# The sign of the gate and value weights: from ScalarE to VectorE

## The chip, the core and the metric
The kernel runs on one core of a Trainium2 chip. TensorE (PE) multiplies matrices; VectorE (DVE), ScalarE (ACT) and GpSimd (POOL) do elementwise work; SyncE (SP) issues the transfers. Each engine takes its instructions strictly in the order of its own program, and waits on semaphores for the others. The metric is the device time of one execution in microseconds (us), lower is better.

## The reference
Three stages follow one another, with `S` = 576 positions, 8 heads of 64, batch 4, thus 2304 tokens of 512:

```python
scores = scale * (q @ k.T);  keep the 32 largest of each row;  attn = softmax of these;  x = attn @ v
x = ((1 / (1 + exp(-(x @ w_gate)))) * (x @ w_val)) @ w_out      # 512 -> 1536 -> 512
h = x @ w_in;  r = maximum(h, 0);  out = (r * r) @ w_out2       # 512 -> 2048 -> 512
```

`q`, `k`, `v` are float32. The five weights come as float64, and there is no float64 arithmetic on the engines: the kernel makes float32 of the two 32-bit words of each number by bit operations.

## The kernel before
**Attention.** The tokens are cut into row blocks of 128; a unit is one head of one block (144 in all). TensorE makes the scores (`sp`), ScalarE copies them (`S`), VectorE finds the 32 largest by four MAX8 (line 389) with three MATCH_REPLACE8 (line 396) between them, ScalarE makes the exponentials (lines 408, 424), VectorE the reciprocal of the sum (`rz`, line 429), TensorE transposes (`tp`, `tq`) and multiplies by the values (`xp`). The first two blocks are chunks 0 and 1, which go through both layers in float32 (`moe32`); later chunks use float16 halves of the weights (`split`).

**Weights.** `conv` takes pairs of 128x512 blocks, 34 pairs: 6 each of gate (`wg`), value (`wv`) and out (`wo`) weights, then 8 each of `wi` and `w2`. For each block: ScalarE scales the high word to float32 (`c`, line 607); VectorE shifts both blocks of `c` by three bits (line 609); ScalarE makes the low word's share (`low`, line 613); the sign is put in; GpSimd adds `low` to `c` (line 623). The sign is put in one of two ways. In a pair whose number divided by `SGN` = 3 leaves 1, ScalarE writes the high word as a float16 zero with its sign into the upper half of `low` (line 616), and the add brings it into `c`. In the other pairs VectorE takes the sign bit out of the high word and ORs it into `c` (line 620). Pairs 1, 4, 7, ... 34 go by ScalarE: two of `wg`, two of `wv`, two of `wo`, three of `wi`, three of `w2`.

**The first MoE step.** When `x_plain` of chunk 0 is there, TensorE makes gate and value of it (`pg`, line 905), ScalarE the tanh (line 914), GpSimd a scale (line 915), VectorE the product `g` (line 917), and TensorE multiplies `g` by the out weights (`acc`, line 927). Beside it run the matmuls of line 640 (`wg_n`: a norm of the weights).

**Order.** Priorities (written into `tc.cur_priority`) and a timeline of estimated durations decide at build time in which order the instructions of each engine stand; the chip then follows that order. So a change of one instruction can move others, on every engine, to the end of the program.

Of the kernel before, what the change touches and what calls it, by code (L numbers as in the profile page):

```python
# [47 lines left out]
SM2 = ()  # L48
XUP = 1000
DIAG = 2  # L50
SGN = 3
SGNS = (1,)
M4RAW = 0
# [21 lines left out]
def tile_topk_attention__then__two_moe_layers(  # L75
# [206 lines left out]
    class Pair:  # L282
# [97 lines left out]
        def softmax(self, j, i, ss, late=None):  # L380
# [48 lines left out]
            nc.vector.reciprocal(rz, bs[:, 3:4])  # L429
            if self.ci < DIAG:  # L430
                dg = apool.tile([P, P], F32, tag="we", bufs=3, name=f"dg_{tt}_{h}")
# [27 lines left out]
        def transpose(self, j, i, wk, dg):  # L459
# [8 lines left out]
            for c in range(CB):  # L468
                o, x = tp[:, c * P : (c + 1) * P], wk[:, c * P : (c + 1) * P]
                if self.ci < DIAG:  # L470

# [3 lines left out]
            nc.scalar.copy(ptr[:, :, i * P : (i + 1) * P], tp.rearrange("p (c t) -> p c t", c=CB))  # L475
            if self.ci < DIAG:
                if i == 0 and j == 0:
# [82 lines left out]
    nblk = [0]  # L560
# [5 lines left out]
    def fetch_to(i):  # L566
        while fetched[0] < len(blocks):
            b = fetched[0]
            spare = b >= len(blocks) - M4RAW
            if b > i and not (b <= i + PREF and (spare or live[0] + 3 <= WSLOTS)):  # L570
                break
            n, kt, fb = blocks[b]
            src = weights[n][kt * P : (kt + 1) * P, fb * 512 : (fb + 1) * 512]
            pool, kw = (mpool, {"tag": "m4", "bufs": M4}) if spare else (wpool, {"tag": "w"})
            if src.dtype == F32:
                t = pool.tile([P, 512], F32, name=f"{n}_r{kt}_{fb}", **kw)
                nc.sync.dma_start(t, src)
            else:
                t = pool.tile([P, 512, 2], U32, name=f"{n}_r{kt}_{fb}", **kw)
                nc.sync.dma_start(t.rearrange("p f t -> p (f t)"), src.bitcast(U32))  # L580
            if not spare:
                live[0] += 1
            raws[(n, kt, fb)] = t
            fetched[0] += 1

    def conv(name, pi):

        pr = pairs_of[name][pi]
        fetch_to(blocks.index((name, *pr[-1])))
        if (name, pi) in CM4:  # L590
            c = mpool.tile([P, 2, 512], F32, tag="m4", bufs=M4, name=f"{name}_c{pi}")
        else:
            c = wpool.tile([P, 2, 512], F32, tag="w", name=f"{name}_c{pi}")
            live[0] += 1
        rs = [raws.pop((name, kt, fb)) for kt, fb in pr]
        ci = c.bitcast(U32)
        wide = weights[name].dtype != F32
        for e, r in enumerate(rs):
            nblk[0] += 1
            if not wide:  # L600
                nc.gpsimd.tensor_copy(c[:, e], r)
            elif YMOD and nblk[0] % YMOD == 0:
                nc.gpsimd.tensor_scalar(
                    c[:, e], r.bitcast(F32)[:, :, 1], REBIAS, 1.0, op0=ALU.mult, op1=ALU.mult
                )
            else:
                nc.scalar.activation(c[:, e], r.bitcast(F32)[:, :, 1], AF.Copy, scale=REBIAS)
        if wide:
            nc.vector.tensor_scalar(ci, ci, 3, None, op0=ALU.logical_shift_left)
            for e, r in enumerate(rs):  # L610
                hi = r[:, :, 1]
                low = r[:, :, 0].bitcast(I32)
                nc.scalar.activation(low, r[:, :, 0], AF.Copy, scale=float(2.0**-29))
                if nblk[0] // 2 % SGN in SGNS:

                    nc.scalar.activation(
                        r.bitcast(F16)[:, :, 1], hi.bitcast(F32), AF.Copy, scale=float(2.0**-60)
                    )
                else:
                    nc.vector.scalar_tensor_tensor(  # L620
                        ci[:, e], hi, 0x80000000, ci[:, e], op0=ALU.bitwise_and, op1=ALU.bitwise_or
                    )
                nc.gpsimd.tensor_tensor(
                    c.bitcast(I32)[:, e], c.bitcast(I32)[:, e], low, op=ALU.add
                )
        live[0] -= sum(blocks.index((name, *b)) < len(blocks) - M4RAW for b in pr)
        for e, (kt, fb) in enumerate(pr):
            flat[(name, kt, fb)] = (c, e)
# [42 lines left out]
    def weight_step(n=1):  # L671
        for _ in range(min(n, len(steps) - nstep[0])):
            name, pi = steps[nstep[0]]
            conv(name, pi)
            nstep[0] += 1
# [607 lines left out]
```

## Time and profile before

| | us |
|---|---|
| median of 3 runs (lowest to highest) | 1274.77 (1273.74 to 1278.67) |
| the profiled execution: its time | 1270.1 |
| its span in the trace | 1267.8 |
| TensorE busy in the span | 1171.9 |
| VectorE, GpSimd, ScalarE busy | 956.3, 844.9, 830.0 |

The profile is that of one execution. The span leaves out some 2.3 us of start and end. A busy time counts an instruction from its start in the record to its end, with what it stalled inside; the records of neighbours overlap a little. A row of a wait names who waited, and after the arrow who came last.

### The profile page before, as it was taken

Reading aid. Unit: us, or ns where it says so; the run is one execution under the profiler, and the core shown is the slowest. Engines: PE = TensorE matmul, PEld = TensorE weight load, DVE = VectorE, ACT = ScalarE, POOL = GpSimd, SP = SyncE. Lnnn points to the kernel's source line nnn. Section 1 sums busy time; section 2 is a strip of 40 time slices with the busy share of each in tenths; the row PEclk is TensorE's granted clock in tenths of the full one; section 3 lists DMA queues with packets and bytes.
Section 4 is the critical chain, followed back from the end, with each engine's and each line's share of the span. In section 5 each row is a group of like instructions: output and inputs, shape, how many; then the busy total and the mean of one; then the engine's idle time right before and its main releaser. Section 6 shows DMA issues by size and latency. Waiting matters only on the chain.

```text
span 1267.8 us, 30670 instructions
## 1 busy us (share of the span) xinstructions
PE 1171.9 (92%) x11477; PEld 952.5 (75%) x11477; DVE 956.3 (75%) x1965; ACT 830.0 (65%) x1719; POOL 844.9 (67%) x1294
## 2 busy tenths in 40 slices
PE   6657889999889989899998999999999999999998
PEld 5436877987777868779786778877886887787775
DVE  6998789899789868889997788998999969210010
ACT  4998996577676766667766676776676757322122
POOL 1788774488776576777875887797688749515223
PEclk9667999999989999999997999999999999999999
DMA  6988763223354346665667465466544623200000
GB/s 183 366 293 284 259 191 85 57 78 88 109 151 118 95 93 147 147 134 119 146 128 155 99 164 120 119 138 154 105 101 92 126 48 67 55 1 1 18 1 17
DMA packets 243188, 153.92 MB, mean 121 GB/s; under 512 B 193120, under 2 KB 209504, under 8 KB 243040
## 3 DMA queue, kind: packets, MB, share of 16 engines
q1 hardware_dynamic: 243040, 151.97, 47.1%
q8 instruction: 90, 1.47, 0.5%
q14 instruction: 58, 0.48, 0.1%
HBM read 105.51 MB, written 18.09 MB: 97 GB/s over the span
## 4 chain that ended last, share of the span: by engine, by line
PE 62%; DVE 14%; ACT 9%; DMA 7%; POOL 5%; issue 3%; SPq 1%; DVEq 0%; POOLq 0%; ACTq 0%
PE ph L851 11%; PE acc L872 10%; PE pv L747 7%; PE pg L747 7%; PE acc L787 6%; PE sp L374 6%; DVE mx L389 5%; DVE W L396 5%; PE xp L506 2%; PE ph L952 2%; DMA PT<-S 2%; DMA kst<-ks 2%; PE acc L969 2%; PE xp L533 2%; PE qpt L334 1%
## 5 line engine op out<-in xcount | busy, mean ns | idle before, releaser
L389 DVE MAX8 mx<-W 128x8 f32<-128x576 f32 x432 | 327.9, 759 | 11.1
L396 DVE MATCH_REPLACE8 W<-mx,W 128x576 f32<-128x576 f32 x288 | 213.8, 742 | 0.0
L851 PE MATMUL ph<-x,wi_w 128*128 128x256 f16 (+1 forms) x1920 | 190.7, 252 | 4.6 <-ACT x L825 3.6
L872 PE MATMUL acc<-w_w,rh 128*128 128x512 f16 x768 | 181.8, 379 | 2.2 <-POOL rh L864 2.2
L851 PEld LDWEIGHTS <-wi_w 128*128 128x128 f16 x1920 | 156.4, 98 | 30.6 <-issue 5.2
L747 PE MATMUL pv<-xs,wv_w 128*128 128x256 f16 (+1 forms) x1440 | 147.0, 254 | 6.0 <-DVE th L759 4.8
L747 PE MATMUL pg<-xs,wg_w 128*128 128x256 f16 (+1 forms) x1440 | 148.2, 253 | 3.1 <-ACT xs L520 2.2
L374 PE MATMUL sp<-kst,qt 128*128 128x288 f32 x608 | 135.3, 335 | 15.7 <-DMA kst<-ks 8.8
L408 ACT ACTIVATE W<-S,mx 128x576 f32<-128x576 f32 x144 | 111.8, 776 | 51.7 <-DVE mx L389 51.4
L454 POOL TENSOR_TENSOR S<-W,S 128x512 f16<-128x512 f32 x192 | 137.0, 736 | 1.6
L747 PEld LDWEIGHTS <-wv_w 128*128 128x128 f16 x1440 | 117.9, 99 | 22.1 <-issue 9.2
L747 PEld LDWEIGHTS <-wg_w 128*128 128x128 f16 x1440 | 118.6, 99 | 17.4 <-issue 1.0
L377 ACT COPY S<-sp 128x576 f32<-128x576 f32 x144 | 92.0, 639 | 57.3 <-PE sp L374 37.5
L872 PEld LDWEIGHTS <-rh 128*128 128x128 f16 x768 | 72.5, 98 | 74.0 <-POOL rh L864 2.8
L787 PEld LDWEIGHTS <-wo_w 128*128 128x128 f16 x1440 | 117.9, 98 | 12.6 <-issue 0.8
L389 DVE MAX8 mx<-S 128x8 f32<-128x576 f32 x144 | 107.3, 745 | 25.0 <-ACT S L377 25.0
L759 DVE TENSOR_TENSOR th<-pv,th 128x512 f32<-128x512 f32 (+1 forms) x60 | 34.5, 576 | 121.3 <-PE pv L747 113.9
L374 PEld LDWEIGHTS sp<-kst,qt 128*128 128x128 f32 x608 | 92.4, 196 | 27.8 <-DMA kst<-ks 8.0
L452 POOL TENSOR_SCALAR W<-W,rz 128x576 f32<-128x576 f32 x96 | 71.9, 749 | 59.8 <-ACT S L451 57.4
L863 POOL TENSOR_TENSOR r<-r 128x512 f32<-128x512 f32 (+1 forms) x80 | 69.6, 871 | 57.4 <-ACT rh L862 51.8
L451 ACT ACTIVATE S<-W,rz 128x576 f16<-128x576 f32 x96 | 74.2, 774 | 50.4 <-DVE rz L447 47.1
L396 DVE MATCH_REPLACE8 W<-mx,S 128x576 f32<-128x576 f32 x144 | 106.9, 743 | 0.3 <-issue 0.3
(290 smaller groups left out, 2349.6 us busy)
## 6 DMA issues: line engine op xcount, KB each, us to landing
kst<-ks SPq DMA_DIRECT2D x112, 288.0 KB, 3.2
v<-vd SPq DMA_DIRECT2D x32, 320.0 KB, 3.4
qn<-in_q_dram SPq DMA_DIRECT2D x128, 64.0 KB, 2.4
wi_r<-in_moe_w_in_dram SPq DMA_DIRECT2D x16, 512.0 KB, 6.1
w_r<-in_moe_w_out_dram SPq DMA_DIRECT2D x16, 512.0 KB, 4.5
v<-in_v_dram SPq DMA_DIRECT2D x56, 128.0 KB, 2.4
wg_r<-in_moe_w_gate_dram SPq DMA_DIRECT2D x12, 512.0 KB, 6.4
wv_r<-in_moe_w_val_dram SPq DMA_DIRECT2D x12, 512.0 KB, 7.0
```

The costliest lines, as they stand in the source:

```text
L374: nc.tensor.matmul(sp[:, e, 0:HALF], l, r, start=(x == 0), stop=(x == len(ops) - 1))
L377: nc.scalar.copy(ss.rearrange("p (e s) -> p e s", e=2), sp[:, :, 0:HALF])
L389: m8 = nc.vector.max(mx[:, r], cur)
L396: nc.vector.match_replace(wk, mx[:, r], cur, NEG)
L408: nc.scalar.activation(wk, ss, AF.Prelu, bias=kth, scale=-1.0, alpha=1.0 / BIG)
L451: nc.scalar.activation(pp[:, 0:S], wk, AF.Copy, scale=rz)
L452: nc.gpsimd.tensor_scalar(wk, wk, rz, 1.0, op0=ALU.mult, op1=ALU.mult)
L454: nc.gpsimd.tensor_tensor(pp[:, o : o + e - f], wk[:, f:e], pp[:, f:e], op=ALU.subtract)
L747: nc.tensor.matmul(pp[:, e * N : (e + 1) * N], wblk(wd, a, c, f0, P), xs[:, b_, c, :], start=(e == 0 and n == 0), stop=(n == 3 * KM - 1), ...
L787: nc.tensor.matmul(accs[d // 2][:, (d % 2) * N : (d % 2 + 1) * N], wblk("wo", a, f, d * P, P), gh[:, b_, e * N : (e + 1) * N], start=(f == ...
L851: nc.tensor.matmul(ph[:, e * N : (e + 1) * N], wblk("wi", a, c, f0, P), x2[:, b_, c, :], start=(e == 0 and n == 0), stop=(n == 3 * KM - 1) ...
L872: nc.tensor.matmul(acc2[i][:, 0:DM], gh[:, b_, e * N + i * P : e * N + (i + 1) * P], wblk("w2", a, f, 0, DM), start=(f == 0 and x == 0), s ...
```

## The change
The sign by ScalarE (line 616 before, 617 after) is kept to the names in a new constant, `wo`, `wi` and `w2`. The four pairs of `wg` and `wv` that had it, eight blocks, take the VectorE way, line 620 before, 621 after.

```diff
--- before.py
+++ after.py
@@ -48,6 +48,7 @@
 SM2 = ()
 XUP = 1000
 DIAG = 2
+SGNW = ("wo", "wi", "w2")
 SGN = 3
 SGNS = (1,)
 M4RAW = 0
@@ -611,7 +612,7 @@
                 hi = r[:, :, 1]
                 low = r[:, :, 0].bitcast(I32)
                 nc.scalar.activation(low, r[:, :, 0], AF.Copy, scale=float(2.0**-29))
-                if nblk[0] // 2 % SGN in SGNS:
+                if name in SGNW and nblk[0] // 2 % SGN in SGNS:
 
                     nc.scalar.activation(
                         r.bitcast(F16)[:, :, 1], hi.bitcast(F32), AF.Copy, scale=float(2.0**-60)
```

ScalarE has eight instructions fewer and VectorE eight more; every other instruction of the program is there as before. All five engines' orders differ in many places from there on. Line numbers of the changed kernel are higher by one.

The first place is VectorE's queue at the first pair of gate weights, in the fourth unit of chunk 0's attention (`wg_c` is the float32 pair, `wg_r` the raw words, `mx`, `S` and `W` the unit's tiles). Before:

```order
L389 MAX mx_3_467<-S_3_327 128x8
L609 TENSOR_SCALAR wg_c_217<-wg_c_217 128x1024
L396 MATCH_REPLACE W_3_466<-mx_3_467,S_3_327 128x576
L389 MAX mx_3_467<-W_3_466 128x8
L396 MATCH_REPLACE W_3_466<-mx_3_467,W_3_466 128x576
L389 MAX mx_3_467<-W_3_466 128x8
```

After:

```order
L390 MAX mx_3_467<-S_3_327 128x8
L610 TENSOR_SCALAR wg_c_217<-wg_c_217 128x1024
L397 MATCH_REPLACE W_3_466<-mx_3_467,S_3_327 128x576
L621 SCALAR_TENSOR_TENSOR wg_c_217<-wg_r_0_205,wg_c_217 128x512
L621 SCALAR_TENSOR_TENSOR wg_c_217<-wg_r_0_207,wg_c_217 128x512
L390 MAX mx_3_467<-W_3_466 128x8
L174 TENSOR_TENSOR kl_3_419<-kpt_3_0_420,kp_3_418 128x512
```

Two sign instructions stand in the softmax of that unit, ahead of its second MAX.

The second place is VectorE's queue ahead of the first product `g` of chunk 0's MoE (`mx_2`, `W_2` are the third unit of chunk 1, `wi_c_1233` and `wi_c_1247` the second and third pairs of `wi`). Before:

```order
L389 MAX mx_2_1121<-S_2_996 128x8
L609 TENSOR_SCALAR wi_c_1233<-wi_c_1233 128x1024
L396 MATCH_REPLACE W_2_1120<-mx_2_1121,S_2_996 128x576
L620 SCALAR_TENSOR_TENSOR wi_c_1233<-wi_r_0_1032,wi_c_1233 128x512
L620 SCALAR_TENSOR_TENSOR wi_c_1233<-wi_r_0_1034,wi_c_1233 128x512
L917 TENSOR_TENSOR g_0_962<-pg_0_942,th_0_959 128x256
L389 MAX mx_2_1121<-W_2_1120 128x8
L173 TENSOR_TENSOR kn_1_964<-kpt_1_0_970,kp_1_969 128x512
L917 TENSOR_TENSOR g_1_1066<-pg_1_1046,th_1_1063 128x256
```

After:

```order
L621 SCALAR_TENSOR_TENSOR wi_c_1233<-wi_r_0_1032,wi_c_1233 128x512
L621 SCALAR_TENSOR_TENSOR wi_c_1233<-wi_r_0_1034,wi_c_1233 128x512
L390 MAX mx_2_1121<-W_2_1120 128x8
L430 RECIPROCAL rz_1_1027<-bs_1_1023 128x1
L397 MATCH_REPLACE W_2_1120<-mx_2_1121,W_2_1120 128x576
L610 TENSOR_SCALAR wi_c_1247<-wi_c_1247 128x1024
L390 MAX mx_2_1121<-W_2_1120 128x8
L174 TENSOR_TENSOR kn_1_964<-kpt_1_0_970,kp_1_969 128x512
L174 TENSOR_TENSOR kn_1_964<-kpt_1_4_977,kp_1_969 128x64
L621 SCALAR_TENSOR_TENSOR wi_c_1247<-wi_r_1_1068,wi_c_1247 128x512
L621 SCALAR_TENSOR_TENSOR wi_c_1247<-wi_r_1_1070,wi_c_1247 128x512
L918 TENSOR_TENSOR g_0_962<-pg_0_942,th_0_959 128x256
```

The rest of that unit's softmax (three MAX, two MATCH_REPLACE), a reciprocal, two key subtractions and the third pair of `wi` (line 609, twice line 620) now stand ahead of `g_0`; they stood behind it.

The third place is TensorE's queue at the first multiplication by the out weights, which reads that `g_0`. Before:

```order
L905 MATMUL pg_1_1046<-x_plain,wv_c_502 128x128 x2
L905 MATMUL pg_1_1046<-x_plain,wv_c_574 128x128 x2
L905 MATMUL pg_1_1046<-x_plain,wv_c_502 128x128 x2
L905 MATMUL pg_1_1046<-x_plain,wv_c_574 128x128 x2
L165 MATMUL kpt_1_0_970<-ident,kn_1_964 128x128 x4
L165 MATMUL kpt_1_4_977<-ident,ke_1_967 128x64
L927 MATMUL acc_0_1198<-g_0_962,wo_c_752 128x128
L640 LDWEIGHTS wg_c_217
```

After:

```order
L166 MATMUL kpt_1_0_970<-ident,kn_1_964 128x128 x4
L166 MATMUL kpt_1_4_977<-ident,ke_1_967 128x64
L906 MATMUL pg_1_1046<-x_plain,wg_c_217 128x128 x2
L906 MATMUL pg_1_1046<-x_plain,wg_c_303 128x128 x2
L906 MATMUL pg_1_1046<-x_plain,wv_c_502 128x128 x2
L906 MATMUL pg_1_1046<-x_plain,wv_c_574 128x128 x2
L906 MATMUL pg_1_1046<-x_plain,wv_c_502 128x128 x2
L906 MATMUL pg_1_1046<-x_plain,wv_c_574 128x128 x2
L473 MATMUL tp_0_1004<-dg_0_912,W_0_896 128x128 x4
L484 MATMUL tq_0_1011<-dg_0_912,W_0_896 64x128
L928 MATMUL acc_0_1198<-g_0_962,wo_c_752 128x128
```

A unit's transposes (`tp`, `tq`) stand ahead of it now; they stood behind it, and the key transposes (`kpt`) went further ahead.

## Rows read from the trace of the kernel before

**Rows 1.** Page, part 1: busy us, share of the span, count, by engine.
```profile
PE 1171.9 (92%) x11477; PEld 952.5 (75%) x11477; DVE 956.3 (75%) x1965; ACT 830.0 (65%) x1719; POOL 844.9 (67%) x1294
```

**Rows 2.** Busy time by stretch: us, PE, PEld, DVE, ACT, POOL, PEclk, DMA share, GB/s.
```profile
34.00:106.00 72.00, 41.55 (x202) 30.72 (x198) 66.53 (x108) 71.81 (x133) 61.78 (x56) 0.62 0.90 314
120.00:191.00 71.00, 63.80 (x579) 56.91 (x579) 56.60 (x120) 63.36 (x116) 53.16 (x54) 0.98 0.73 232
```

**Rows 3.** The chain that ended last, 34 to 87 us, by line.
```profile
by line: ACT wv_r L613 11.3%; ACT wg_r L613 11.1%; PE xp L533 10.0%; ACT wv_c L607 8.8%; ACT wg_c L607 8.7%; ACT wv_r L616 6.8%; DMA kst<-ks 6.5%; ACT W L408 6.4%; ACT wg_r L616 6.2%; ACT W L424 5.7%; issue 4.6%; ACT PT L475 3.5%; ACT S L37
```

**Rows 4.** Groups by line, whole span: busy us, mean ns, idle before.
```profile
L620 DVE SCALAR_TENSOR_TENSOR wo_c<-wo_r,wo_c 128x512 uint32<-128x512 uint32 x8 | 8.4, 1085 | 0.1
...
L609 DVE TENSOR_SCALAR wv_c<-wv_c 128x1024 uint32<-128x1024 uint32 x6 | 7.2, 1194 | 0.2 <-ACT wv_c L607 0.2
...
L609 DVE TENSOR_SCALAR wg_c<-wg_c 128x1024 uint32<-128x1024 uint32 x6 | 6.4, 1059 | 1.2 <-ACT wg_c L607 1.2
...
L620 DVE SCALAR_TENSOR_TENSOR wv_c<-wv_r,wv_c 128x512 uint32<-128x512 uint32 x8 | 6.0, 776 | 0.0
...
L620 DVE SCALAR_TENSOR_TENSOR wg_c<-wg_r,wg_c 128x512 uint32<-128x512 uint32 x8 | 5.9, 779 | 0.0
...
L616 ACT ACTIVATE wg_r<-wg_r 128x512 f16<-128x512 f32 x4 | 5.4, 1360 | 0.0
...
L616 ACT ACTIVATE wv_r<-wv_r 128x512 f16<-128x512 f32 x4 | 5.3, 1382 | 0.0
```

**Rows 5.** Lines 620, 609, 34 to 120 us: ns min/median/max, starts.
```profile
L620 DVE SCALAR_TENSOR_TENSOR wo_c<-wo_r,wo_c x8: 668/712/1785, 91.8 to 109.6; 128x512 uint32<-128x512 uint32 x8
...
L609 DVE TENSOR_SCALAR wo_c<-wo_c x6: 674/904/1790, 84.9 to 107.0; 128x1024 uint32<-128x1024 uint32 x6
```

**Rows 6.** VectorE's instructions in order of time, 117 to 126 us.
```profile
118.46 0.41 DVE L917 TENSOR_TENSOR g<-pg,th 128x256 f32<-128x256 f32 x1
...
118.80 0.74 DVE L389 MAX8 mx<-W 128x8 f32<-128x576 f32 x1
...
120.05 0.41 DVE L917 TENSOR_TENSOR g<-pg,th 128x256 f32<-128x256 f32 x1
...
124.61 0.76 DVE L389 MAX8 mx<-W 128x8 f32<-128x576 f32 x1
```

**Rows 7.** VectorE's waits, 30 to 120 us: total, times, longest.
```profile
DVE rz L429 <- POOL bs L428: 3.4, 1, 3.4
...
DVE wg_c L609 <- ACT wg_c L607: 1.2, 1, 1.2
...
DVE kl L173 <- ACT kp L172: 1.2, 1, 1.2
```

**Rows 8.** TensorE's instructions in order of time, 113 to 125 us.
```profile
118.93 0.49 PE L927 MATMUL acc<-g,wo_c 128*128 128x128 f32 x2 [4.73 <-DVE g L917]
...
123.57 1.10 PE L472 MATMUL tp<-dg,W 128*128 128x128 f32 x8
...
124.60 0.43 PE L483 MATMUL tq<-dg,W 128*64 128x128 f32 x2
```

**Rows 9.** TensorE's waits, 120 to 191 us.
```profile
PE acc L927 <- DVE g L917: 2.6, 1, 2.6
...
PE wv_cb L648 <- DVE wv_d L646: 1.9, 1, 1.9
...
PE xp L533 <- ACT PE L484: 0.8, 1, 0.8
...
PE wo_cb L648 <- DVE wo_d L646: 0.6, 1, 0.6
```

**Rows 10.** VectorE's waits, 120 to 191 us.
```profile
DVE w_c L609 <- ACT w_c L607: 6.4, 3, 3.7
...
DVE wi_c L609 <- ACT wi_c L607: 6.3, 2, 4.4
```

**Rows 11.** Busy time by stretch, later ones with idle TensorE.
```profile
300.00:380.00 80.00, 71.23 (x849) 62.71 (x848) 65.43 (x133) 60.02 (x139) 58.44 (x97) 0.94 0.44 125
440.00:540.00 100.00, 86.32 (x1211) 72.84 (x1209) 78.59 (x186) 67.27 (x166) 71.27 (x130) 1.00 0.59 131
660.00:700.00 40.00, 33.84 (x310) 28.15 (x308) 31.80 (x73) 26.76 (x59) 23.34 (x41) 0.83 0.72 157
```


## The prediction
> **What bounds the kernel now.** I read the busy times first. TensorE is busy 92% of the span, VectorE 75%, ScalarE 65% [rows 1], so as a whole TensorE sets the time, and an edit on the other two counts only through the time that TensorE stands idle. Then the stretches. The edited instructions lie between 30 and 75 us, in a stage where it is the other way round: from 34 to 106 us ScalarE is busy 71.8 of 72.0 us, VectorE 66.5, GpSimd 61.8, TensorE 41.6 at a mean granted clock of 0.62, a mixture of the 1.2 and the 2.4 GHz level [rows 2]. From 120 to 191 us TensorE is busy 63.8 of 71.0. The chain of work that ended last, from 34 to 87 us, is a string of ScalarE's instructions, and the signs of line 616 are in it with 6.8% and 6.2% of 53 us, some 7 us [rows 3]. So this stage hangs on ScalarE, with VectorE right behind it. What TensorE gets from it is the start of chunk 0's MoE: it waits 4.73 us for the first product `g` before its matmul at 118.93 [rows 8]. From there on it has work nearly all the time.
>
> **The change, part by part.**
> *Removed from ScalarE.* Eight instructions of 1.36 to 1.38 us (the means of `wg` and `wv` [rows 4]): 10.9 to 11.1 us less in that queue. Taken alone this would pay, since the chain runs there.
>
> *Added to VectorE.* Eight instructions of line 620. The same form on the same weights takes 0.776 to 0.779 us in the mean [rows 4], so 8 x 0.78 = 6.2 us. Bounds: the shortest of that line is 0.668, the longest 1.785 [rows 5]; that makes 5.3 to 14.3. I take the mean, which comes from the same place of the program.
>
> *Cover for it.* VectorE's waits between 30 and 120 us are one of 3.4, one of 1.2 and one of 1.2 us [rows 7]. The two short ones are for ScalarE's lines 607 and 172, which stood behind signs that are gone: I count both as taken. The long one is a reciprocal's, released by GpSimd; its place in the queue moved too, and I count half. Together 4.1 us; bounds 0 and 5.8.
>
> *Moved.* Ahead of the first `g` in VectorE's queue there are now also eleven rows that stood behind it (second place of the order above). In the trace they run from the MAX at 118.80 to the end of the one at 124.61 + 0.76, which is 6.6 us, less some 0.4 for the second `g` between them: 6.2 us [rows 6]. VectorE is late there already, since TensorE waits for it. So `g` ends 6.2 + 6.2 - 4.1 = 8.3 us later, and with it the wait of 4.73 us grows. What is queued behind the waiting matmul on TensorE is the norm of the weights and the rest of chunk 0's MoE.
>
> *Given back at once.* TensorE has the transposes `tp` and `tq` ahead of that wait now instead of behind it: 1.10 + 0.43, 1.5 us [rows 8]. Left: 6.8 us.
>
> *Given back up to 191 us.* TensorE's idle time from 120 to 191 us is 71.0 - 63.8 = 7.2 us [rows 2]. Waits for VectorE make 2.6 + 1.9 + 0.6 = 5.1 of it, the longest for ScalarE 0.8 [rows 9]. A TensorE that comes 6.8 us later finds these done, if VectorE and ScalarE don't come later too. They don't: the eleven rows are then behind VectorE, which leaves it 8.3 - 6.2 = 2.1 us late, and it had 6.4 + 6.3 us of waits for ScalarE's line 607 in that stretch [rows 10], which shrink with 10.9 us less ahead of them on ScalarE. I count 5.1 + 0.8 = 5.9 us as given back; bounds 0 and 7.2. The signs issue no transfers, and a raw block is read last by GpSimd's add in either way, so no slot comes free later through them alone.
>
> *Sum.* 6.8 - 5.9 = 0.9 us later at 191 us, and TensorE carries that to the end. Against the profiled execution's own time, 1270.1 us, that is 1271.0. That execution lies 4.7 us below the median of the runs, 1274.77; on that scale I predict **1275.7 us**. With all bounds at one end the sum runs from 5.3 + 6.2 - 5.8 - 1.5 - 7.2 = -3.0 to 14.3 + 6.2 - 0 - 1.5 - 0 = +19.0 us.
>
> **What the skill says against it.** VectorE's line 620 varies between 0.668 and 1.785 us on one form, and its line 609 between 0.674 and 1.790 [rows 5]; so something holds it up beside GpSimd's adds, which fill much of the same stretch. The Trainium skill (SBUF — State Buffer, "SBUF: two separate sides") says that VectorE and GpSimd have one pair of ports in common, which an instruction holds as a whole, and that a VectorE instruction with two inputs in SBUF asks for it against a GpSimd one that reads SBUF; the rows agree with that. By it the eight new instructions could each stand behind an add, which is the slower rival. The Trainium skill (Perfetto Trace Analysis, "Optimizing Scalar/DVE Operations") also advises to move work to ScalarE where VectorE is saturated; this change goes the other way, at 92% against 99.7% busy, and by that advice nothing would be gained.
>
> **The rivals.**
> *Slower: VectorE's queue is held up further and TensorE doesn't get it back.* Place: VectorE from 40 to 126 us. If the eight signs take 1.085 us, as the eight of `wo` do in the mean [rows 4], the lag of `g` grows by 2.5 to 10.8 us; after `tp` and `tq` 9.3 are left, and with nothing given back up to 191 us the time is 1274.77 + 9.3 = 1284.1 us. For it: the mean of `wo` and the longest of 1.785. Against it: the 12.7 us of VectorE's waits for ScalarE behind that place [rows 10]. It decides from the point at which more than 6.4 us of the lag are left at 191 us.
>
> *Faster: ScalarE was the bound, and VectorE's stalls go.* Over the shortest of their lines, VectorE's instructions stall for 6 x (1.059 - 0.674) + 6 x (1.194 - 0.674) us in line 609 of `wg` and `wv`, and 8 x 0.11 + 8 x 0.11 + 8 x 0.42 us in line 620: 2.3 + 3.1 + 0.9 + 0.9 + 3.3 = 10.5 us [rows 4, 5]. If GpSimd's adds, fed earlier by ScalarE, slip to other times, part of that goes, `g` comes sooner than I count, and TensorE saves at the wait of 4.73 us and behind it. All of it would give 1275.7 - 10.5 = 1265.2 us; it is over 0.5% from 7.3 us of the 10.5 on, 1268.4. For it: the chain on ScalarE [rows 3]. Against it: the number of adds is the same and VectorE has more to do among them.
>
> *The order further on.* The engines' orders differ to the end of the program. TensorE idles 80.0 - 71.2 = 8.8 us between 300 and 380, 13.7 between 440 and 540 and 6.2 between 660 and 700, where the granted clock is 0.94, 1.00 and 0.83 [rows 11]: 28.7 us, which hang on what stands next to what, and nothing in the trace says which way they go. A third more or less is 9.6 us: 1285.3 or 1266.1.
>
> That the signs don't move is excluded: eight rows of line 616 are gone from ScalarE's queue and eight have come to VectorE's.
>
> **How the numbers follow.** What a measurement of this kernel can tell from no change is about 0.5%, 6.4 us. The likeliest case, a lag that is mostly given back, has 0.56 and holds everything from 1268.4 to 1281.1. The slower rival has 0.15, the faster one 0.13, the order further on 0.16, half to each side. That gives faster 0.21, same 0.56, slower 0.23. The range leaves out about a tenth on each side: it reaches to the full price of the faster rival, 1265, and past that of the slower one and of the order, 1286.
>
> **What would show it right or wrong.** Right: ScalarE's busy time falls by about 11 us and VectorE's rises by 5 to 9; the first line 918 starts near 127 us instead of 118.46, TensorE's wait there is longer than 4.73 us, and its idle time from there to 191 us falls from 7.2 us to 2 or less; at 191 us TensorE is within 3 us of before. The slower rival shows signs of over 1 us and idle time for VectorE behind 127 us, the faster one a `g` before 121 us and shorter lines 610 and 621. If TensorE's busy and idle time up to 300 us is as before and the total is not, the order further on did it, and my sum, which stops at 191 us, is wrong in leaving it out.

## The result, and the profile after

The change is slower: 1286.1 us in the median of six runs (1282.93 to 1288.36), against 1274.59 for the kernel before (six runs, 1271.27 to 1278.67). The ratio is 1.0089, 95% interval 1.0070 to 1.0108, so about 11.5 us. That is at the upper edge of the forecast range, which the text puts at 1286, and not the case that was called likeliest. The profiled execution took 1287.04 us with a span of 1285.3; that of before, 1270.1, lies 4.5 us under the median, so differences of single profiles are good to some 4 us only, and the sizes below are taken from ratios where there are any.

The page's busy times (us, share, instructions), and the busy time by stretch (us, then TensorE, its weight loads, VectorE, ScalarE, GpSimd, granted clock, DMA share, GB/s) of the change:

```profile
PE 1180.0 (92%) x11477; PEld 959.2 (75%) x11477; DVE 966.0 (75%) x1973; ACT 823.8 (64%) x1711; POOL 840.9 (65%) x1294
```

```profile
34.00:106.00 72.00, 35.42 (x156) 26.69 (x155) 71.40 (x113) 60.66 (x116) 61.74 (x52) 0.57 0.87 307
120.00:191.00 71.00, 59.83 (x528) 54.91 (x527) 58.40 (x115) 60.51 (x108) 50.49 (x50) 0.90 0.71 226
300.00:380.00 80.00, 70.66 (x759) 59.74 (x757) 66.17 (x126) 59.63 (x127) 58.72 (x93) 0.94 0.41 112
440.00:540.00 100.00, 89.91 (x1229) 78.84 (x1227) 80.63 (x192) 69.01 (x168) 68.11 (x128) 0.95 0.57 122
```

Against [rows 1, 2] ScalarE lost 11.1 us of work between 34 and 106 us, and VectorE, at 66.5 before, is now busy 71.4 of 72.0 there: the two have changed places. (ScalarE has 17 instructions fewer in that stretch, not only the eight signs; over the whole span its busy time fell by 6.2 us.) From 120 to 191 us TensorE is idle 11.2 us instead of 7.2, and its granted clock is 0.90 instead of 0.98. The chain of work that ended last, by line from 34 to 87 us, shows the same swap; in [rows 3] it was ScalarE's:

```profile
by line: DVE mx L390 20.4%; DVE wv_c L621 18.9%; DVE W L397 17.6%; issue 16.2%; DVE wg_c L621 12.9%; DVE wg_c L610 4.6%; DVE wv_c L610 3.9%; DVE wo_c L610 2.0%; DVE kl L174 1.5%; ACT wg_r L614 1.3%; ACT kp L173 0.9%; DVE rz L430 0.6%; ACT x
```

The groups of line 621 (line 620 before; busy us, mean ns, idle before) and VectorE's waits from 30 to 120 us (total, times, longest):

```profile
L621 DVE SCALAR_TENSOR_TENSOR wv_c<-wv_r,wv_c 128x512 uint32<-128x512 uint32 x12 | 10.4, 906 | 0.0
...
L621 DVE SCALAR_TENSOR_TENSOR wg_c<-wg_r,wg_c 128x512 uint32<-128x512 uint32 x12 | 9.0, 787 | 0.0
```

```profile
DVE wg_c L610 <- ACT wg_c L608: 0.9, 1, 0.9
DVE kl L174 <- ACT kp L173: 0.4, 1, 0.4
```

The eight signs added 10.4 + 9.0 - 6.0 - 5.9 = 7.5 us [rows 4], and 5.8 us of waits [rows 7] shrank to 1.3. VectorE and TensorE in order of time behind that place (start, us, idle time before and its releaser):

```profile
117.86 1.81 DVE L610 TENSOR_SCALAR wi_c<-wi_c 128x1024 uint32<-128x1024 uint32 x1
...
125.14 0.80 DVE L174 TENSOR_TENSOR kn<-kpt,kp 128x512 fp32r<-128x512 f32 x2
125.86 1.28 DVE L621 SCALAR_TENSOR_TENSOR wi_c<-wi_r,wi_c 128x512 uint32<-128x512 uint32 x2
127.06 0.41 DVE L918 TENSOR_TENSOR g<-pg,th 128x256 f32<-128x256 f32 x1
...
136.63 0.29 DVE L647 TENSOR_TENSOR wg_d<-wg_n,ident 128x128 bf16<-128x128 f32 x1 [1.38 <-PE wg_n L641]
```

```profile
125.95 2.05 PE L473 MATMUL tp<-dg,W 128*128 128x128 f32 x8 [5.48 <-DVE kn L174]
127.93 0.69 PE L484 MATMUL tq<-dg,W 128*64 128x128 f32 x2
128.55 0.80 PE L928 MATMUL acc<-g,wo_c 128*128 128x128 f32 x2
```

The first product `g` comes 8.6 us later than in [rows 6]. The transposes `tp`, which I had counted as work that TensorE does while it waits, wait themselves: 5.48 us for `kn`, another of the rows in the same queue. But the inputs of `g` come later too. The last copy of chunk 0's `x_plain`, with which its MoE begins, and GpSimd's scale of `th`, a factor of `g`, before:

```profile
105.69 0.27 ACT L541 COPY x_plain<-xp 128x128 f32<-128x128 f32 x1
115.90 0.84 POOL L915 TENSOR_SCALAR th<-th 128x256 f32<-128x256 f32 x1
```

And after:

```profile
111.81 0.27 ACT L542 COPY x_plain<-xp 128x128 f32<-128x128 f32 x1
123.97 0.84 POOL L916 TENSOR_SCALAR th<-th 128x256 f32<-128x256 f32 x1
```

`x_plain` is 6.1 us late and `th`, done at 124.8 instead of 116.7, 8.1 us. What TensorE's idle time does next is in the stretches behind it:

```profile
122.00:127.00 5.00, 1.05 (x5) 1.08 (x6) 5.00 (x10) 2.00 (x3) 3.78 (x6) 0.84 0.58 165
125.95:130.95 5.00, 5.00 (x21) 4.26 (x22) 3.04 (x5) 5.00 (x11) 4.27 (x4) 0.50 0.74 220
181.63:186.63 5.00, 5.00 (x23) 5.00 (x24) 4.97 (x11) 3.37 (x5) 2.79 (x4) 0.50 0.87 215
```

TensorE stands idle for 4 of 5 us, and in the 5 us behind the wait it is busy throughout at a granted clock of 0.50, the 1.2 GHz level. So part of the stall is paid a second time, as work at half the clock. The kernel before pays some of that too, behind its wait of 4.73 us. The larger difference is at the last product `g` of chunk 0's first layer (third line above, second line below); the two stretches before are:

```profile
118.93:123.93 5.00, 5.00 (x32) 4.66 (x33) 5.00 (x13) 2.39 (x5) 3.57 (x5) 0.66 0.87 290
175.59:180.59 5.00, 5.00 (x40) 4.71 (x41) 4.97 (x12) 4.23 (x9) 3.30 (x4) 1.00 0.82 230
```

That last `g` and the matmuls that read it, before:

```profile
175.12 0.41 DVE L917 TENSOR_TENSOR g<-pg,th 128x256 f32<-128x256 f32 x1
175.59 2.05 PE L927 MATMUL acc<-g,wo_c 128*128 128x128 f32 x16 [2.55 <-DVE g L917]
```

And after:

```profile
181.16 0.41 DVE L918 TENSOR_TENSOR g<-pg,th 128x256 f32<-128x256 f32 x1
181.63 3.78 PE L928 MATMUL acc<-g,wo_c 128*128 128x128 f32 x16 [3.44 <-DVE g L918]
```

VectorE is 6.0 us late there, TensorE waits longer than before, and the same 16 matmuls take 3.78 us instead of 2.05. The copy that ends this layer starts at 185.45 us instead of 177.68, 7.8 us later. TensorE's waits from 120 to 191 us:

```profile
PE tp L473 <- DVE kn L174: 5.5, 1, 5.5
PE acc L928 <- DVE g L918: 4.9, 2, 3.4
PE wo_cb L649 <- DVE wo_d L647: 0.8, 1, 0.8
```

Two marks divide the rest: the copy that ends chunk 1's first MoE layer (line 946, 945 before, its second instruction), and the seventh maximum `x2cm` (line 822, 821 before). The change reaches them at:

```profile
285.86 0.59 ACT L946 COPY x_plain<-acc 128x512 f32<-128x512 f32 x1 [0.67 <-PE acc L928]
```

```profile
940.65 0.42 DVE L822 TENSOR_REDUCE x2cm<-x2pq 128x1 f32<-128x256 f32 x1 [3.57 <-PE x2pq L820]
```

The kernel before is there at 277.55 and 925.50: it is 8.3 us ahead at the first mark and 15.2 at the second, in profiles whose spans differ by 17.5. Something costs before 280 us, and something again behind it.

### The profile page after: what moved, and what is told of

It is laid out like the page before. It is cut to its first block, busy times and chain, and to the rows that moved or that the text cites. A ratio compares the mean times of both kernels' runs of the same rounds, so it can differ in the third digit from the quotient of the medians.

```text
span 1285.3 us, 30677 instructions
## 1 busy us (share of the span) xinstructions
PE 1180.0 (92%) x11477; PEld 959.2 (75%) x11477; DVE 966.0 (75%) x1973; ACT 823.8 (64%) x1711; POOL 840.9 (65%) x1294
## 4 chain that ended last, share of the span: by engine, by line
PE 60%; DVE 18%; POOL 7%; DMA 5%; issue 4%; ACT 3%; SPq 2%; POOLq 0%; DVEq 0%; ACTq 0%
PE acc L873 9%; PE ph L852 9%; PE acc L788 8%; PE pg L748 7%; PE pv L748 7%; DVE mx L390 7%; DVE W L397 6%; PE sp L375 5%; PE xp L507 3%; PE ph L953 2%; PE acc L970 2%; DMA PT<-S 2%; PE xp L534 2%; DMA kst<-ks 1%; PE qpt L335 1%
## 5 line engine op out<-in xcount | busy, mean ns | idle before, releaser
L390 DVE MAX8 mx<-W 128x8 f32<-128x576 f32 x432 | 327.9, 759 | 10.6
L788 PE MATMUL acc<-gh,wo_w 128*128 128x256 f16 (+1 forms) x1104 | 107.8, 251 | 2.5 <-POOL gh L764 1.5
```

The lines of the kernel that those rows point to most:

```text
L390: m8 = nc.vector.max(mx[:, r], cur)
L788: nc.tensor.matmul(accs[d // 2][:, (d % 2) * N : (d % 2 + 1) * N], wblk("wo", a, f, d * P, P), gh[:, b_, e * N : (e + 1) * N], start=(f == ...
```

## The experiments

**Theories.** A: VectorE's queue. What stands ahead of the first `g` there delays TensorE, and the lag is carried to the end. B: the order further on. A scheduler places the instructions by durations that it assumes, so moving eight of them rearranges every engine to the end of the program, and some arrangements run worse. C: each sign on VectorE costs its share by its load. All ratios are to the kernel before, on the same chip, with their 95% intervals.

**The two halves.** One name more stays in the tuple:

```diff
-SGNW = ("wo", "wi", "w2")
+SGNW = ("wg", "wo", "wi", "w2")
```

> Only value's four signs go to VectorE (gate's four stay on ScalarE). In VectorE's queue the four stand ahead of the first product g and one other row more than before. Theory A (the lag of g: what VectorE has more ahead of the first g is carried to the end nearly whole, as in the change, where g came 8.6 us later and the end 11.5): 4 x 0.8 + 0.7 less the 4.1 us of waits that cover it, so g 0 to 1 us later, and the time 1273 to 1277 us against 1274.6. Theory B (the order further on: the engines' orders beyond 300 us decide, whatever g does): the orders differ here too, so the time is off by 5 us or more, to either side, with g on time. Theory C (the load: each sign on VectorE costs its share, 11.5 / 8 us): 1280 us.

1276.63 us, 1.0022 (1.0004 to 1.0039). Of this run only the times are used. The other half has `"wv"` in place of `"wg"`:

> Only gate's four signs go to VectorE (value's four stay on ScalarE). The work moved is that of the run with value's four, but ahead of the first product g stand the four and some nine other rows more than before. Theory A (the lag of g): 4 x 0.78 + 9 x 0.6 - 4.1 = 4.4 us later at g, and the time 1278 to 1281 us. Theory B (the order further on): no relation of the time to g's lag. Theory C (each sign on VectorE costs its share): 1280 us, as with value's four alone; so the two halves together tell A from C.

1281.93 us, 1.0072 (1.0050 to 1.0095). The halves differ, so C falls. A's lag of `g` fits (4.5 us for 4.4) and the time lies 0.9 us over A's range, but at the first mark this kernel is at 278.84, only 1.3 us behind before; the rest of its 8 us arose later.

**Relief and load apart.** The eight signs are done by nobody, or ScalarE keeps them and VectorE does eight idle ones besides:

```diff
-                else:
+                elif name in SGNW or nblk[0] // 2 % SGN not in SGNS:
                     nc.vector.scalar_tensor_tensor(
```

> The eight signs of gate and value are left out: neither ScalarE nor VectorE does them, so those weights have no sign bit. ScalarE has its 10.9 us less, VectorE no sign more, though five more other rows (some 3.5 us) stand ahead of the first product g. Theory A: 3.5 less the up to 5.8 us of VectorE's waits that less work on ScalarE shortens: g between 3 us sooner and 1 later, and the time 1270 to 1276 us. Theory B: 5 us or more to either side while g is within 3 us. If ScalarE was the bound of that stage and VectorE's queue only followed, g comes 5 us or more sooner and the time is under 1269 us.

1277.33 us, 1.0031 (1.0013 to 1.0049): slower with less work. It is 6.6 us ahead of before at the first mark (270.92) and 4.4 behind it at the second (929.89). That points to B, with 11 us.

```diff
                 if nblk[0] // 2 % SGN in SGNS:
                     nc.scalar.activation(...)
+                    if name in ("wg", "wv"):
+                        nc.vector.scalar_tensor_tensor(
+                            ci[:, e], hi, 0, ci[:, e], op0=ALU.bitwise_and, op1=ALU.bitwise_or
+                        )
```

> ScalarE keeps all its signs as before, and VectorE does eight more instructions of the sign's form on the same pairs, with a mask of zero, so that they change nothing. No other row moves ahead of the first product g. Theory A: 8 x 0.8 = 6.4 us more, of which VectorE's waits cover 2 to 4 us (ScalarE is as late as before): g 2 to 5 us later, the time 1277 to 1281 us. Theory C (each sign on VectorE costs its share, 11.5 us): 1286 us. Theory B: no relation to g's lag, 5 us or more off from what g says.

1274.14 us, 1.0005 (0.9988 to 1.0022). `g` starts at 120.92, 2.5 us later than before, within what A gives for eight signs and no rows moved; but the time is 3 us under A's range: the lag was not carried on. The last copy of `x_plain` is at 110.66, 5.0 us late, with no row moved ahead. The eight instructions as such are nearly free. The eleven rows that come with them in the change are not in this run.

**The same work in other orders.** Other values of the planner's numbers `MUP` and `CA` rearrange the program and leave the work alone. Among them are runs in which VectorE, ScalarE and GpSimd follow one order, row for row, from some 240 us of their traces on, and that differ in the signs.

```diff
-MUP = 200.0
+MUP = 160.0
```

> The kernel before with one planner number changed (40 instead of 200 less 40: the MoE steps' lead, 160 for 200); the work and the 139 rows of VectorE's queue up to the first product g are those of before. From VectorE's row 309 on, some 210 us, each engine's order is the one of the run with load on VectorE alone. Theory A (the lag of g): g as before, so within 3 us of 1273.8. Theory B (the order further on decides): this order gave 1274.1 us with eight more instructions on VectorE and g 5.3 us later, so without them 1269 to 1274 us; only the order moves it against before.

1271.70 us, 0.9998 (0.9975 to 1.0020). This order costs nothing. The change in it:

```diff
-CA = 6.0
+CA = 5.9
 SGNW = ("wo", "wi", "w2")
```

> The change, with the planner's cost of an attention step at 5.9 instead of 6.0: VectorE's queue up to the first g has the change's 158 rows, the same eight signs and eleven others ahead, but from VectorE's row 322 on each engine's order is, row for row, that of the run of before in the other order. So the two differ by the change's own work and its lag at g alone. Theory A (the lag of some 8 us is carried to the end): 8 us above the run of before in the other order, 1279 to 1283 us. Theory B (the lag is given back, and the order further on made the change slow): within 3 us of the run of before in the other order, 1271 to 1276 us. Half of each would be 1276 to 1279 us.

1277.93 us, 1.0047 (1.0031 to 1.0063). Neither theory alone: 6.2 us over the run beside it, as A says, and 0.42% less than the change, as B says. From mark to mark the two, and the change, look like this (columns as above):

```profile
279.71:923.59 643.88, 609.29 (x6905) 503.97 (x6904) 565.97 (x1205) 455.36 (x1018) 483.15 (x835) 0.99 0.53 127
```

```profile
285.08:931.62 646.54, 608.98 (x6905) 503.23 (x6904) 566.25 (x1204) 454.86 (x1018) 483.14 (x835) 0.99 0.53 126
```

```profile
285.86:940.65 654.79, 619.54 (x6910) 509.91 (x6909) 566.17 (x1205) 459.06 (x1021) 482.56 (x839) 0.98 0.55 125
```

In one order before's work and the change's take 643.9 and 646.5 us; the 5.4 us between them are there at the first mark (279.71 against 285.08). In its own order the change takes 8 us more, and TensorE's idle time is not what grew (35.3 against 37.6 us): its busy time is, by 10.6 us on all but the same instructions, at a lower mean clock.

**Before's work, the change's later order.** `MUP = 202.0` in the kernel before:

> The kernel before with the planner's number at 202 for 200: work and the rows up to the first g as before (the first 181 of VectorE's), but VectorE's last 617 rows, from some 550 us on, and ScalarE's, GpSimd's and TensorE's with them, stand in the order of the change; between the two places the order is a third one. Theory A: g as before, so within 3 us of 1273.8. Theory B: the change lost some 7 us behind 300 us through its order, and the same order costs it here too: 1278 to 1283 us.

1276.85 us, 1.0032 (1.0017 to 1.0047): slower by order alone, with `g` at 118.14. In its trace VectorE follows the change's order from some 670 us on, not from 550; at the third maximum `x2cm` (525.2 us, 518.4 before) 4.9 of the 5.7 us are lost that it loses from mark to mark. So it shows that an order has a price, not that this one is the change's. From mark to mark it takes 653.6 us with TensorE busy 620.5:

```profile
279.41:933.03 653.62, 620.52 (x6903) 510.44 (x6902) 564.98 (x1206) 458.00 (x1022) 484.76 (x839) 0.97 0.54 125
```

**The opposite choice.** `SGNW = ("wg", "wv", "wo")`:

> The other half of the choice: the twelve signs of the second layer's two weights go from ScalarE to VectorE, and gate's, value's and the out weight's stay on ScalarE. They lie behind 120 us, where VectorE had 12.7 us of waits for ScalarE; ScalarE loses 12 x 1.37 = 16.4 us, VectorE gains 12 x 0.78 = 9.4. Theory A: g is not touched and VectorE's waits cover the rest, so 1270 to 1275 us, or less if TensorE's waits there for VectorE (5.1 us) go. Theory B: the order further on changes until the last third of the program, so up to 10 us to either side with g as before.

1283.92 us, 1.0100 (1.0078 to 1.0122), far from what A let me expect. Part of it looks like A's mechanism at another place: from 120 to 191 us VectorE is busy 67.1 us where it was 56.6 [rows 2], and TensorE at a clock of 0.89 has a longer wait for it, 5.6 us where it was 0.2. At the first mark the kernel is 6.5 us behind before; another 7.9 come between the marks, and what of them is the order's was not separated.

```profile
120.00:191.00 71.00, 61.01 (x531) 55.43 (x531) 67.10 (x129) 50.69 (x103) 50.20 (x52) 0.89 0.73 237
```

```profile
PE wg_cb L649 <- DVE wg_d L647: 5.6, 1, 5.6
```

**Halves and relief in known orders.** Value's four with `MUP = 202`, gate's four with `MUP = 160` and with `CA = 5.9`, and the relief with `MUP = 195`:

> Value's four signs alone on VectorE, as in the run that cost 0.22%, with a planner's number (MUP 202 for 200) by which VectorE's last 1226 rows, from some 200 us on, stand in the order of the kernel before, and so do TensorE's but for a few. If that run's 0.22% were due to the order further on, this one is at 0.0% (within 2 us of before) or faster, if the relief of ScalarE by 5.5 us is worth something. If the moved signs themselves cost it, 0.2% again.

1275.86 us, 1.0003 (0.9989 to 1.0017). Value's four cost nothing in before's order.

> Gate's four signs alone on VectorE, with a planner's number (MUP 160 for 200) by which VectorE's last 1224 rows, from some 200 us on, stand in the order of the change. With the lag of gate's four (1.3 us at 280 us in the earlier run) and the change's order further on (some 5 us): 0.4 to 0.6% over before. If the order were worth nothing: 0.1%.

1279.39 us, 1.0025 (1.0011 to 1.0040), under the 0.4 to 0.6% that the order's price let me expect.

> The same work as the run beside it, gate's four on VectorE, but (CA 5.9 for 6.0) VectorE's last 1221 rows stand in the order of the run of before in the other order, which cost 0.0%. With a lag of 1.3 us and no price of the order: 0.0 to 0.2% over before, some 5 us less than in the change's order. If the order were worth nothing, the two are alike.

1277.02 us, 1.0008 (0.9986 to 1.0030). The order's price is there in the middle values, 2.4 us, but the intervals overlap; taken from this pair alone it is open. Between the marks the two take 655.95 and 649.34 us, again with TensorE's busy time, 619.24 and 612.63, making the difference.

> The eight signs of gate and value left out, as in the run of ScalarE's relief alone (those weights have no sign bit), with a planner's number (MUP 195 for 200) by which the last 617 rows of VectorE, from some 550 us on, stand in the order of before. The earlier run was 6.6 us ahead at 280 us and lost 11 behind it. If its order behind 550 us took them: 0.3 to 0.5% faster than before, 1266 to 1269 us. If the loss lies between 280 and 550 us: 0 to 0.3% slower, as in the earlier run.

1269.11 us, 0.9936 (0.9916 to 0.9957). Less work on ScalarE is worth 8 us here and cost 4 in the order that its first run had. The profiles don't show where: the profiled execution took 1271.94 us, some 3 over the median here, and 1273.98, some 3 under it, there.

The profiles at the two marks (us; the last column is TensorE's busy time between them):

| work | later order | first mark | mark to mark | TensorE busy |
|---|---|---|---|---|
| before | its own | 277.55 | 647.95 | 613.00 |
| value's four | before's | 277.13 | 651.57 | 612.99 |
| before | the other | 279.71 | 643.88 | 609.29 |
| load alone | the other | 280.51 | 648.08 | 612.82 |
| gate's four | its own | 278.84 | 658.23 | 620.24 |
| gate's four | the other | 281.13 | 649.34 | 612.63 |
| the change | the other | 285.08 | 646.54 | 608.98 |
| gate's four | the change's | 277.84 | 655.95 | 619.24 |
| the change | its own | 285.86 | 654.79 | 619.54 |
| before | third, then the change's | 279.41 | 653.62 | 620.52 |
| the second layer's twelve | its own, then before's | 284.01 | 655.88 | 616.39 |
| relief alone | its own | 270.92 | 658.97 | 616.07 |
| relief alone | its own, then before's | 268.85 | 657.09 | 612.35 |

The first mark goes with the work ahead of it: four signs leave it where it was (277.1 to 281.1), eight with the eleven rows put it 5 to 8 us later, the relief 7 to 11 sooner. In the second column the change's order stands apart, 654.8 and 656.0 us against 643.9 to 651.6 for before's and the other; within one order single profiles differ by up to 5.5.

The four runs in the other order give the lag in steps; up to some 240 us their orders differ. The copy is the one that ends chunk 0's first layer:

| work | first `g` | copy | `g` later by | copy later by |
|---|---|---|---|---|
| before | 117.77 | 182.25 | | |
| load alone | 120.92 | 181.63 | 3.15 | -0.62 |
| gate's four | 123.13 | 183.45 | 5.36 | 1.20 |
| the change | 127.50 | 187.41 | 9.73 | 5.16 |

Of each lag some 4 us (3.8, 4.2, 4.6) are back when the layer ends, and only what is over that stays. The times follow: 0.9998, 1.0005, 1.0008 and 1.0047.

## Why the prediction was wrong in its sum, and right only at the edge of its range

**Right.** The cover of 4.1 us (measured 4.5), and `g` at 127.06 for the "near 127" forecast. The signs cost 7.5 us for 6.2, inside their bounds. Right behind that place VectorE caught up as worked out: at `wg_d` it is 1.3 us behind before (136.63 against 135.31), for a forecast 2.1, and its waits for line 607 (now 608), 12.7 us in [rows 10], are 1.7 in its waits from 120 to 191 us:

```profile
DVE wi_c L610 <- ACT wi_c L608: 1.5, 3, 0.6
...
DVE w_c L610 <- ACT w_c L608: 0.2, 1, 0.2
```

**Right in size by luck: the 8.3 us at `g`.** The sum takes 6.2 of them from the eleven rows ahead of `g`. In the trace `th` is ready at 124.8 us only, so that with those rows out of the way `g` could still not start before that: at most 2.3 of the 8.6 us are theirs directly, and perhaps 1.4 more through two of them that stand ahead of the signs of the pair that GpSimd adds just before `th`. Most of the rest lies ahead of the MoE, where `x_plain` is 6.1 us late behind a VectorE that is now the chain. The range too was reached without its reason: the slower rival and the order stand in it as alternatives, at 1284.1 and 1285.3, and what came was a part of each.

**The step that failed is "Given back up to 191 us", 5.9 us.** It rests on the premise that VectorE and ScalarE don't come later too. At the layer's last `g` VectorE is 6.0 us late, not 2.1, and the layer ends 7.8 us late, for 0.9 in the sum. Behind its first wait TensorE's idle time up to 191 us is 11.2 - 5.5 = 5.7 us, for 7.2 before: 1.5 us came back, not 5.9. The clock, for which the sum had no term, takes more than that: an estimate from the mean granted clocks, 0.90 and 0.98 at two levels, 1 and 0.5, is 2 x 0.10 x 71.0 = 14.2 us at the lower level against 2 x 0.02 x 71.0 = 2.8; half of the difference, 5.7 us, is lost. The 1.5 us "given back at once" came to nothing, since the wait is now at `tp`. With the order behind 240 us held equal, `g` is 9.7 us late, some 4.6 come back by the end of the layer for 7.4 in the sum (1.5 + 5.9), 5.4 are left at the first mark, and the time differs by 6.2. From there on the lag was carried to the end, as the sum has it.

**The sum left out a second term.** The order behind some 240 us makes 1.0089 against 1.0047, 0.42% or 5.4 us, and their intervals don't overlap. It was named as a rival, but priced from the wrong thing: a third of TensorE's idle time. It arises in TensorE's busy time; from 440 to 540 us, for one, the idle time fell from 13.7 us [rows 11] to 10.1, at a granted clock of 0.95 for 1.00. The change's 0.89% is thus parted into 0.47 for the lag and 0.42 for the order.

**The rivals.** The slower one (VectorE's queue held up, nothing given back) had the right place; of its 9.3 us 6.0 came, and not by slower signs, which took 0.79 and 0.91 us in the mean for its 1.085. The faster one has something true in it: relief of ScalarE alone is worth 8 us, in one of two orders. It falls here because VectorE had the chain as soon as ScalarE gave it up, and the eight signs, nearly free beside a ScalarE that was the bound (1.0005), were then in the chain. The Trainium skill (Perfetto Trace Analysis, "Optimizing Scalar/DVE Operations") says that handing work to ScalarE may make sense where VectorE is saturated; the runs agree in that both moves the other way were slower, 1.0089 here and 1.0100 for the second layer's weights, with the order's share in both.

**Open.** How much of the late `x_plain` is the signs' and how much that of other rows in the new order was not separated; no run has the rows ahead without the signs. Which of the rearranged matmuls lets the clock fall between the marks was not traced to an instruction. Of the versions that do all of the work none beats the kernel before by more than its interval.

## What to carry to other kernels

Where one engine is the bound at 99.7% and the next is at 92%, moving work to the next one swaps them: price it by the second engine's own waits, and follow the inputs of the step that it delays, not only the queue ahead of it. Idle time further on is slack only where the engines waited for don't come later themselves; some 4 us came back here, whatever the lag, and a wait of TensorE costs the lower clock behind it besides. Where a scheduler sets the order, run an edit in two or three orders, and the old work in them too: here order alone was worth 0.4%, about as much as the lag that the edit itself made.

## What the runs showed of the hardware

TensorE's busy time on the same matmuls differs with their order. The pages (one profile each) of the change in the other order, and of before in the third order:

```profile
PE 1167.9 (92%) x11477; PEld 950.9 (75%) x11477; DVE 969.1 (76%) x1973; ACT 821.3 (64%) x1711; POOL 846.2 (66%) x1294
```

```profile
PE 1183.7 (93%) x11477; PEld 961.7 (75%) x11477; DVE 955.3 (75%) x1965; ACT 831.2 (65%) x1719; POOL 842.1 (66%) x1294
```

Most of the 15.8 us lies between the marks, 620.5 - 609.0 = 11.5, where the mean granted clock is 0.97 against 0.99. With two levels, 1 and 0.5, that is an estimated 2 x 0.03 x 653.6 = 39 us at the lower level against 2 x 0.01 x 646.5 = 13; half of the difference is 13 us, so the clock accounts for it within the rounding. For the change in its two orders (0.98 and 0.99) the same estimate gives 6.6 of 10.6 us; the rest is open. Within one order the column goes from 609.0 to 612.8. The stretches behind TensorE's waits show the size of single pieces: 5 us at 0.50 behind 5.48 us of waiting and again behind 3.44, and 0.66 over 5 us behind 4.73 us in the kernel before.
